# Half-height turns of k and q, q loaded eight tokens per row, and loads that wait for the fifth last

## The chip, the core and the metric

The kernel runs on one core of a Trainium2 chip. The core has a matrix engine (TensorE, PE in the profile; its weight loads are shown apart as PEld), a vector engine (VectorE, DVE), a scalar engine (ScalarE, ACT), a general engine (GpSimd, POOL) and a queue engine (SyncE, SP), which issues nearly all DMA transfers here. TensorE reads SBUF and writes PSUM, eight banks of 2 KB in each of 128 partitions; VectorE and ScalarE copy from PSUM to SBUF.

The metric is the device time of one execution, in microseconds (us), as the median of several runs. A profile is taken from one execution of its own.

## What is computed

A decayed linear attention in blocks of 64 tokens (4 batches, 8 heads, 768 tokens, 64 channels), and a highway layer on its output with the heads side by side (3072 tokens, 512 features):

```python
intra = np.einsum('bhic,bhjc->bhij', qb, kb) * Dmask[None]
intra = np.einsum('bhij,bhjd->bhid', intra, vb)
inter = np.einsum('bhid,bhde->bhie', qb * lam_pow[None], kv_state)
out[:, :, sl] = intra + inter
kv_state = lam_block[None, :, None, None] * kv_state + np.einsum('bhsd,bhse->bhde', kb_dec, vb)
...
H = np.maximum(x @ w_h, 0.0)
T = 1.0 / (1.0 + np.exp(-(x @ w_t + b_t)))
return (T * H + (1.0 - T) * x).astype(np.float32)
```

## The kernel before

The kernel works with chunks of 128 tokens in place of the 64 of the reference. The decay is split: q is multiplied by lam to the power of the token's position, v by its inverse, and a 0/1 mask (tri) is left between them. Two chunks are one superblock, n = 0 to 11, three to a batch.

The order of all work is written out by hand in PLAN (lines 17 to 60), a list of tokens. A loop at lines 384 to 388 reads each token and issues its instructions, so each engine gets its instructions in the order of the list. A token is name.arguments, with "=" before the PSUM banks and "@" before the engine. In the list:

- Lk, Lq, Lv (load, line 170): 256 KB of k, q or v, four heads of a superblock, on SP's queue. A partition holds two neighbouring tokens of each head, so one piece of a transfer is 512 bytes. W (line 176) loads a half of a weight matrix, in rows of 2 KB. WC casts it.
- CK, CQ, CV (lines 183, 193, 196): the cast of k to bf16, and the scaling of q and v with their powers. A last argument of 2 means all eight heads, 0 or 1 four of them.
- TK, TQ (trans, line 199): for each pair of heads and each of the two token parities, one 128 x 128 transpose on TensorE into one PSUM bank. EK, EQ (lines 206, 210) copy the 1024 columns out to kT and qT.
- S, SS (lines 236, 224): the scores, in 64 x 64 tiles of TensorE. SS mixes them with U, the state matmuls (line 219). KE copies the state out of PSUM. M (line 254) masks the scores on VectorE.
- I and A (lines 265, 276): the two parts of the attention's output, o. D (take, line 285) copies o out to xT. Its columns are in the order of parity, and the copy puts them in token order with a permuted write.
- F (block, line 295): eight matmuls of the highway layer, 256 tokens wide. H, G, X (lines 303, 308, 316): relu, sigmoid, gate.
- R (turns, line 340): turns of the result to token rows, in tiles of 64 rows; E copies them out, ST stores them through SP's queue. The last superblock goes in two chunks, with turn (line 321).
- Z (spin, line 362): matmuls without use that keep TensorE busy. PT (line 381) loads the sigmoid's table. B and BC make a column of the bias.

Each load needs a free buffer; there are five each of kf, qf and vf (BUFS, line 62). SP works its transfers in order, so a store whose data is not there yet holds the loads behind it. There is no other limit on transfers in flight.

Of the kernel before, what the change touches and what calls it, by code (L numbers as in the profile page):

```python
# [29 lines left out]
R.1=40 H.2.1 SS.3.1=62 Lv.5.0 F.2.0.0=3 CK.4.2@POOL KE.3.0@ACT M.3.1.1 Lv.5.1 E.1.1@ACT M.3.1.0 SS.3.0=52 E.1.0@ACT  # L30
H.2.0 Lq.6.0 TQ.4.2=0 KE.3.1@ACT CV.4.2@POOL M.3.0.1 TK.4.2=6 G.2.1@ACT Lq.6.1 F.2.0.1=4 M.3.0.0 EQ.4.2@ACT EK.4.2@DVE
Lv.6.0 I.3=32 A.3.0 CK.5.2@POOL A.3.1 Lk.6.1 SS.4.1=56 D.3.0@ACT D.3.1@DVE TK.5.2=0 KE.4.0@ACT M.4.1.1 Lk.6.0
F.3.0.0=2 G.2.0@ACT CQ.5.2@POOL EK.5.2@DVE Lv.6.1 SS.4.0=36 H.3.0 F.3.0.1=0 Lq.8.0 M.4.0.0 CV.5.2@POOL M.4.0.1
TQ.5.2=2 Lk.9.0 G.3.0@ACT F.3.1.0=3 X.2.1@DVE Lq.7.0 EQ.5.2@ACT X.2.0@DVE F.3.1.1=6 CQ.6.2@POOL M.4.1.0 Lq.7.1
KE.4.1@ACT I.4=14 H.3.1 G.3.1@ACT R.2=25 Lk.8.1 X.3.0@DVE A.4.0 E.2.1@ACT X.3.1@DVE A.4.1 Lk.7.1 SS.5.0=30 E.2.0@ACT
D.4.0@DVE CK.6.2@POOL SS.5.1=56 D.4.1@ACT Lk.7.0 TQ.6.2=2 M.5.0.0 KE.5.0@ACT CV.6.2@POOL TK.6.2=1 M.5.1.1 Lv.7.0
EQ.6.2@ACT F.4.1.0=4 M.5.0.1 Lv.7.1 EK.6.2@ACT F.4.0.0=3 H.4.1 Lk.8.0 M.5.1.0 I.5=62 SS.6.1=01 H.4.0 Lq.8.1 A.5.0
KE.6.0@ACT M.6.1.0 CQ.7.2@POOL R.3=45 Lv.9.1 A.5.1 M.6.1.1 SS.6.0=30 D.5.0@ACT Lv.8.0 F.4.0.1=1 M.6.0.0 D.5.1@ACT
M.6.0.1 Lk.9.1 TQ.7.2=6 G.4.0@ACT CK.7.2@POOL F.5.0.0=3 Lq.10.1 EQ.7.2@ACT F.4.1.1=2 H.5.0 Lk.10.1 E.3.1@ACT X.4.0@DVE
TK.7.2=0 CV.7.2@POOL G.4.1@ACT I.6=63 ST.0 KE.6.1@DVE F.5.0.1=5 X.4.1@DVE Lv.8.1 F.5.1.0=1 G.5.0@ACT CK.8.2@POOL  # L40
EK.7.2@DVE Lq.9.0 A.6.0 E.3.0@ACT H.5.1 A.6.1 SS.7.1=20 Lq.9.1 D.6.0@ACT D.6.1@DVE TK.8.2=4 M.7.1.1 F.6.1.0=1 Lv.9.0
EK.8.2@ACT X.5.0@DVE CK.9.2@POOL F.6.1.1=6 KE.7.0@DVE Lk.10.0 CQ.8.2@POOL H.6.1 R.4=30 SS.7.0=54 Lk.11.1 E.4.0@ACT
F.5.1.1=1 E.4.1@ACT M.7.0.1 G.6.1@ACT ST.4 M.7.1.0 TK.9.2=3 Lq.10.0 M.7.0.0 TQ.8.2=0 G.5.1@ACT CV.8.2@POOL F.6.0.0=4
EQ.8.2@DVE Lk.11.0 KE.7.1@ACT X.5.1@DVE I.7=25 EK.9.2@ACT Lq.11.0 A.7.0 H.6.0 A.7.1 CQ.9.2@POOL SS.8.0=01 X.6.1@DVE
D.7.1@ACT Lv.10.1 SS.8.1=34 M.8.0.1 D.7.0@ACT F.6.0.1=6 KE.8.0@DVE Lq.11.1 CK.10.2@POOL F.7.0.0=5 M.8.1.0 G.6.0@ACT
M.8.1.1 ST.3 TQ.9.2=1 CV.9.2@POOL H.7.0 F.7.1.0=2 EQ.9.2@ACT Lv.10.0 X.6.0@DVE TK.10.2=3 M.8.0.0 ST.1 I.8=45
EK.10.2@ACT CQ.10.2@POOL H.7.1 SS.9.1=61 A.8.1 KE.9.0@ACT M.9.1.0 A.8.0 R.5=02 M.9.1.1 SS.9.0=36 CK.11.2@POOL
E.5.1@DVE F.7.0.1=1 KE.9.1@ACT M.9.0.1 E.5.0@ACT F.7.1.1=2 D.8.0@DVE D.8.1@ACT ST.5 CQ.11.2@POOL M.9.0.0 G.7.0@ACT
Lv.11.1 TK.11.2=6 Lv.11.0 I.9=04 F.8.1.0=5 EK.11.2@ACT ST.2 X.7.0@DVE TQ.10.2=3 G.7.1@ACT H.8.1 CV.10.2@POOL F.8.0.0=1
EQ.10.2@ACT R.6=65 H.8.0 A.9.1 X.7.1@DVE A.9.0 SS.10.1=31 D.9.0@ACT D.9.1@DVE F.8.1.1=2 E.6.1@ACT M.10.1.1 F.9.1.0=0  # L50
E.6.0@DVE G.8.1@ACT M.10.1.0 ST.6 TQ.11.2=4 CV.11.2@POOL KE.10.0@DVE F.9.1.1=5 EQ.11.2@ACT X.8.1@DVE SS.10.0=16
G.9.1@ACT H.9.1 R.7=32 M.10.0.1 KE.10.1@ACT F.8.0.1=4 X.9.1@DVE E.7.0@ACT M.10.0.0 E.7.1@ACT I.10=06 SS.11.0=53
G.8.0@ACT ST.7 A.10.0 M.11.0.0 A.10.1 SS.11.1=21 D.10.1@ACT X.8.0@DVE F.9.0.0=5 KE.11.0@ACT M.11.1.0 D.10.0@ACT
F.9.0.1=6 M.11.0.1 M.11.1.1 F.10.1.0=4 G.9.0@ACT H.9.0 I.11=20 X.9.0@DVE A.11.0 A.11.1 R.8=31 D.11.0@ACT R.9=56
E.8.0@ACT F.10.0.0=2 E.9.0@DVE E.9.1@ACT E.8.1@ACT D.11.1@DVE ST.9 F.10.1.1=3 H.10.0 ST.8 F.10.0.1=6 H.10.1 G.10.1@ACT
F.12.1.1=5 G.10.0@ACT X.10.1@DVE F.11.1.1=1 F.11.1.0=0 G.12.1@ACT X.10.0@DVE F.11.0.1=2 G.11.1@ACT H.11.1 F.12.1.0=4
R.10=36 G.11.0@ACT H.12.1 X.11.1@DVE F.11.0.0=0 E.10.0@ACT X.12.1@DVE F.12.0.1=4 E.10.1@ACT H.11.0 F.12.0.0=1
G.12.0@ACT X.11.0@DVE ST.10 R.11.1.1=5 H.12.0 R.11.0.2=3 E.11.1.1@DVE X.12.0@DVE E.11.0.2@ACT ST.11.1.1 R.11.1.0=0
ST.11.0.2 E.11.1.0@DVE ST.11.1.0
"""  # L60

BUFS = dict(kf=5, qf=5, vf=5, kb=3, qb=2, vs=3, kT=2, qT=2, m=8, xT4=2, th4=2, xT2=3, xT1=2, th2=2, th1=2, hm2=3, hm1=2, tb2=2, tb1=2, ss=4, o=5, oh=2, oq=1)
# [3 lines left out]
def kernel(  # L66
# [13 lines left out]
    C = 128  # L80
# [4 lines left out]
    J = 2  # L85
    N = B * NST
# [12 lines left out]
    def copy(eng, dst, src):  # L99
        if eng == "ACT":  # L100
            A.activation(dst, src, AF.Copy)  # L101
        else:
            ENG[eng].tensor_copy(dst, src)  # L103
# [62 lines left out]


    SRC = {"k": k, "q": q, "v": v}

    def load(x, n, p, eng):  # L170
        b, c = divmod(n, NST)
        hs = heads(p)
# [246 lines left out]
```

## Time and profile before

| | |
|---|---|
| median of 7 runs | 109.19 us (108.9 to 111.0) |
| the profiled execution | 109.75 us |
| its span, first to last instruction | 107.7 us |
| TensorE busy, granted clock | 99.3 us, 0.998 |
| VectorE, ScalarE, GpSimd busy | 82.4, 71.8, 55.6 us |
| moved by DMA | 27.59 MB in 42701 packets, 256 GB/s mean |
| loads of k, q, v | 24 each, 5.3, 5.6, 5.4 us to landing (median) |

Busy times overlap between engines, and a busy engine is not always at its peak. The span is the profiled execution's own; what lies around it is not in the trace. In a list of groups, a row gives line, engine, operation, output and inputs with their shapes, the count, then the busy time in us and the mean of one in ns, then the idle time of the engine ahead of them and what ended it. In the chain by time, a row gives start, duration, and what ran.

### The profile page before, as it was taken

How to read it: one execution, taken by the hardware profiler on the slowest of the kernel's cores; microseconds unless marked ns; L12 is line 12 of the kernel's file. 1: busy time of each engine (PE TensorE's matmuls, PEld its weight loads, DVE VectorE, ACT ScalarE, POOL GpSimd, SP SyncE). 2: the span in 40 equal slices, each digit the busy share in tenths (PEclk: the TensorE clock that was granted, in tenths of full speed). 3: DMA queues.
4: the chain of work that ended last, by engine and by line, in shares of the span. 5: the costliest groups of instructions: out<-in, count | busy, mean ns of one | idle time of the engine just before them, and what ended most of it. 6: DMA issues, size and time to landing. Idle time of an engine off the chain costs nothing.

```text
span 107.7 us, 4970 instructions
## 1 busy us (share of the span) xinstructions
PE 99.3 (92%) x2190; PEld 80.5 (75%) x2190; DVE 82.4 (77%) x140; ACT 71.8 (67%) x129; POOL 55.6 (52%) x46
## 2 busy tenths in 40 slices
PE   4986999999999999999999999998899999999950
PEld 1332665588987888889889889896698888899930
DVE  1233495879798797999995996999577998958860
ACT  3304254686875598499679758978197798687940
POOL 6028340427989877889548396998193060000000
PEclk9999999999999999999999999999999999999999
DMA  0899999999999999999999999999749454108264
GB/s 3 231 303 291 291 355 389 321 288 268 279 304 287 301 280 293 280 291 282 293 290 300 308 359 303 338 313 344 257 169 277 161 202 163 42 6 318 78 242 147
DMA packets 42701, 27.59 MB, mean 256 GB/s; under 512 B 1588, under 2 KB 38712, under 8 KB 42680
## 3 DMA queue, kind: packets, MB, share of 16 engines
q1 hardware_dynamic: 42528, 27.27, 86.6%
q8 instruction: 17, 0.28, 1.2%
q14 instruction: 4, 0.03, 0.1%
q10 hardware_dynamic: 152, 0.01, 0.1%
HBM read 20.98 MB, written 6.29 MB: 253 GB/s over the span
## 4 chain that ended last, share of the span: by engine, by line
PE 78%; DVE 6%; DMA 5%; issue 3%; POOL 1%; SPq 1%; ACT 1%; POOLq 0%; DVEq 0%
PE bt L300 19%; PE bh L300 18%; PE bs L216 8%; PE bo L281 6%; PE bx L347 6%; PE bqtr L204 6%; DMA qf<-in_q_dram 5%; PE bktr L204 5%; PE bspin L366 5%; PE bo L271 4%; DVE m L255 4%; PE kv L221 2%; POOL qb L190 1%; DVE hm L305 1%; SPq L173 1%
## 5 line engine op out<-in xcount | busy, mean ns | idle before, releaser
L300 PEld LDWEIGHTS <-w_b 128*128 128x128 bf16 x416 | 36.4, 98 | 4.5
L255 DVE TENSOR_TENSOR m<-bs,tri 128x512 bf16<-128x512 f32 x48 | 31.0, 679 | 2.2 <-PE bs L216 1.9
L190 POOL TENSOR_TENSOR qb<-qf,pow_q 128x1024 bf16<-128x1024 f32 (+1 forms) x13 | 23.5, 1809 | 11.1 <-DMA qf<-in_q_dram 11.1
L314 ACT ACTIVATE bt<-bt,bt_col 128x256 f32<-128x256 f32 (+1 forms) x52 | 22.0, 432 | 5.6 <-PE bt L300 2.9
L300 PE MATMUL bh<-xT,w_b 128*128 128x256 bf16 (+1 forms) x208 | 25.0, 265 | 0.0
L300 PE MATMUL bt<-xT,w_b 128*128 128x256 bf16 (+1 forms) x208 | 24.5, 265 | 0.0
L190 POOL TENSOR_TENSOR vs<-vf,pow_v 128x1024 bf16<-128x1024 f32 x10 | 19.0, 1902 | 7.2 <-DMA vf<-in_v_dram 6.2
L305 DVE SCALAR_TENSOR_TENSOR hm<-bh,xT 128x512 bf16<-128x512 f32 (+1 forms) x26 | 16.5, 643 | 3.7 <-PE bh L300 2.2
L318 DVE TENSOR_TENSOR th<-bt,hm 128x512 bf16<-128x512 f32 (+1 forms) x26 | 16.4, 642 | 2.1 <-ACT bt L314 2.0
L101 ACT ACTIVATE xT<-bo 128x512 bf16<-128x512 f32 x16 | 11.6, 750 | 4.2 <-PE bo L281 4.2
L216 PE MATMUL bs<-qT,kT 64*64 64x128 bf16 x384 | 13.8, 218 | 0.3
L366 PE MATMUL bspin<-blank,id 128*128 128x512 bf16 x45 | 12.6, 424 | 1.4 <-POOL id masks.py:199 1.4
L101 ACT ACTIVATE ss<-kv 128x512 bf16<-128x512 f32 x15 | 8.9, 596 | 7.2 <-PE bs L216 6.0
L103 POOL CAST kb<-kf 128x1024 bf16<-128x1024 f32 (+1 forms) x10 | 9.9, 994 | 7.3 <-DMA kf<-in_k_dram 6.6
L216 PEld LDWEIGHTS <-kT 64*64 64x64 bf16 x384 | 10.9, 106 | 2.6 <-issue 1.1
L101 ACT ACTIVATE o<-bx 128x512 f32<-128x512 f32 x19 | 10.4, 596 | 1.4 <-PE bx L347 1.3
L101 ACT ACTIVATE qT<-bqtr 128x1024 bf16<-128x1024 bf16 (+1 forms) x10 | 9.8, 981 | 1.8 <-PE bqtr L204 1.8
L281 PE MATMUL bo<-m,vs 64*64 64x128 bf16 x384 | 9.3, 219 | 1.5 <-issue 1.1
L366 PEld LDWEIGHTS <-id 128*128 128x128 bf16 x45 | 4.4, 107 | 6.8 <-issue 2.2
L221 PE MATMUL kv<-vs,kb 64*64 64x64 bf16 x320 | 9.1, 196 | 0.0
L281 PEld LDWEIGHTS <-vs 64*64 64x64 bf16 x384 | 6.5, 106 | 3.3 <-issue 2.4
L204 PE MATMUL bqtr<-id,qb 128*128 128x128 bf16 x96 | 7.5, 220 | 0.9 <-POOL qb L190 0.9
(50 smaller groups left out, 109.0 us busy)
## 6 DMA issues: line engine op xcount, KB each, us to landing
kf<-in_k_dram SPq DMA_DIRECT2D x24, 256.0 KB, 5.3
vf<-in_v_dram SPq DMA_DIRECT2D x24, 256.0 KB, 5.4
qf<-in_q_dram SPq DMA_DIRECT2D x24, 256.0 KB, 5.6
out_dram<-o SPq DMA_DIRECT2D x11, 512.0 KB, 4.4
w_f<-in_moe_w_h_dram SPq DMA_DIRECT2D x2, 512.0 KB, 6.6
w_f<-in_moe_w_t_dram SPq DMA_DIRECT2D x2, 512.0 KB, 8.6
out_dram<-oh SPq DMA_DIRECT2D x2, 128.0 KB, 2.0
out_dram<-oq SPq DMA_DIRECT2D x1, 256.0 KB
```

Of the source, the lines that this page charges most:

```text
L101: A.activation(dst, src, AF.Copy)
L190: ENG[eng].tensor_tensor(dst, in0=get(src, n)[:, heads(p)].rearrange("p h (j d) -> p h j d", j=J), in1=pw[:, n % NST, heads(p), :, None].t ...
L204: T.transpose(t[:, i, j, :], get(x + "b", n)[:, j, h:h + 2, :], id128)
L216: T.matmul(get("s", n, e, hp // 2)[half(b), hp % 2, j, :], lhsT=get("kT", n)[half(e), hp, j, half(b)], rhs=get("qT", n)[half(e), hp, :, ha ...
L221: T.matmul(kv[half(e), hp, half(e)], lhsT=get("kb", n)[half(b), j, 2 * hp + e, :], rhs=get("vs", n)[half(b), 2 * hp + e, j, :], start=firs ...
L255: V.tensor_tensor(new(("m", n, e, u), [128, 2, J, C]), in0=get("s", n, e, u), in1=tri[:, None].to_broadcast([128, 2, J, C]), op=ALU.mult)
L281: T.matmul(get("o", n, b)[half(e), hp, :], lhsT=get("vs", n)[half(b), 2 * hp + e, j, :], rhs=get("m", n, e, u)[half(b), hp % 2, j, :], sta ...
L300: T.matmul(t[:, r, :], lhsT=w_b[w][:, kc, (2 * u + r) * 128:(2 * u + r + 1) * 128], rhs=get("xT", *g)[:, kc, :], start=(kc == 0), stop=(kc ...
L305: V.scalar_tensor_tensor(new(("hm", g, u), [128, 2, z * C], tag=f"hm{z}"), in0=get("h", g, u), scalar=0.0, in1=get("xT", *g)[:, 2 * u:2 * ...
L314: A.activation(dst[:, r, :], src[:, r, :], AF.Sigmoid, bias=bt_col[:, 2 * u + r:2 * u + r + 1])
L318: ENG[eng].tensor_tensor(new(("th", g), [128, NP, z * C], tag=f"th{z}")[:, 2 * u:2 * u + 2, :], in0=get("tt", g, u), in1=get("hm", g, u), ...
L366: T.matmul(t, lhsT=id128, rhs=blank, start=True, stop=True)
```

## The change

- A turn's input is now 64 rows (one chunk, b) instead of 128, so that there are twice as many, of half the size, alternating between the upper and the lower half of TensorE's rows. k and q of a superblock are turned by one token T, into two banks, one for each chunk; each bank holds k and q. A bank is copied out by ET (evac_t) with one copy for k and one for q, 512 columns each. TK and TQ stay for the first superblock, which is done in halves.
- q is loaded in rows of eight tokens: partition (o, h) holds tokens 8o to 8o+7 of the heads 2h and 2h+1, and one piece of a transfer is 2 KB. A load is one head parity; both are needed ahead of CQ. The powers for q are made anew for that layout (two small DMA and arithmetic steps at the start).
- The copy of q out of PSUM reads in runs of four and puts the columns in token order, four head pairs side by side for each token. So the moving operand of the scores and of I steps by four elements. With q in token order, o is too: D is a plain copy, and the mask is made for that order.
- All transfers on SP go through dma, which from the 15th on makes each wait for the fifth last.
- PLAN is written anew: other places, engines and banks of the tokens throughout. The engine counts: KE 20 on ScalarE (15 and 5 on VectorE before), ET 15 on ScalarE and 11 on VectorE, D 13 and 11 (16 and 8), E of whole superblocks 15 and 7 (19 and 3). The spins are 47 instead of 45. PT comes ahead of the first turn.

```diff
+    lam_bc = singles.tile([128, H + 2], F32)
+    A.dma_start(out=lam_bc[:, 0:H], in_=lam.partition_broadcast(128))
+    A.dma_start(out=lam_bc[:, H:H + 2], in_=lam.rearrange("(h x) -> h x", x=2)[None].to_broadcast([32, NP, 2]))
...
+    issued = []
+
+    def dma(dst, src, eng=None):
+        i = (eng or nc.sync).dma_start(out=dst, in_=src)
+        if len(issued) >= 14:
+            tc.add_manual_dep(i.ins, issued[-5].ins.name,
+                              mybir.DependencyInfo(mybir.DependencyClass.Sync, mybir.DependencyReason.DATA), reason="few transfers at a time")
+        issued.append(i)
 
     def load(x, n, p, eng):
         b, c = divmod(n, NST)
+        ts = slice(c * 2 * C, (c + 1) * 2 * C)
+        if x == "q":
+            dst = new(("qf", n), [128, 2, Q * D], F32)
+            dma(dst[:, p], q[b, :, ts, :].rearrange("(h x) (o j) d -> x o h (j d)", x=2, j=Q)[p])
+            return
...
+    def cast_q(n, p, eng):
+        js = slice(0, Q) if p == 2 else slice(4 * p, 4 * p + 4)
+        z = js.stop - js.start
+        ENG[eng].tensor_tensor(new(("qb", n), [128, Q, 2, D])[:, js].rearrange("p j x d -> p x j d"),
+                               in0=get("qf", n).rearrange("p x (j d) -> p x j d", j=Q)[:, :, js],
+                               in1=pow_q[:, n % NST, :, js, None].to_broadcast([128, 2, z, D]), op=ALU.mult)
...
-    def trans(x, n, p, bk):
+    def trans(xs, n, p, bk):
         hs = heads(p)
-        t = bank((x + "tr", n, p), bk[0], [128, (hs.stop - hs.start) // 2, J, C], BF16)
-        for i, h in enumerate(range(hs.start, hs.stop, 2)):
-            for j in range(J):
-                T.transpose(t[:, i, j, :], get(x + "b", n)[:, j, h:h + 2, :], id128)
...
+        for b, i in enumerate(bk):
+            bank(("tr", n, p, b), i, [128, 2, (hs.stop - hs.start) // 2 * C // 2 * J], BF16)
+        if "k" in xs:
+            t = [get("tr", n, p, b)[:, 0].rearrange("p (h j i) -> p h j i", j=J, i=C // 2) for b in range(2)]
+            for i, h in enumerate(range(hs.start, hs.stop, 2)):
+                for j in range(J):
+                    for b in range(2):
+                        T.transpose(t[b][:, i, j, :], get("kb", n)[half(b), j, h:h + 2, :], id128[half(b), half(b)])
+        if "q" in xs:
+            t = [get("tr", n, p, b)[:, 1].rearrange("p (j i) -> p j i", i=C // 2) for b in range(2)]
+            for i in range(Q if p == 2 else Q // 2):
+                for b in range(2):
+                    T.transpose(t[b][:, i, :], get("qb", n)[half(b), i + (4 if p == 1 else 0)], id128[half(b), half(b)])
+
+    def evac_t(n, p, b, eng):
+        es = slice(0, 512) if p == 2 else slice(256 * p, 256 * p + 256)
+        js = slice(0, Q) if p == 2 else slice(4 * p, 4 * p + 4)
+        dst, src = new(("T", n), [128, 2, 2, 512], tag="kT")[:, b], get("tr", n, p, b)
+        copy(eng, dst[:, 0, es], src[:, 0])
+        copy(eng, dst[:, 1].rearrange("p (i j h) -> p i j h", j=Q, h=NP)[:, :, js],
+             src[:, 1].rearrange("p (j i h) -> p i j h", i=16, h=NP))
+
+    def kT(n, b, hp):
+        return get("T", n)[:, b, 0].rearrange("p (h j i) -> p h j i", h=NP, j=J)[:, hp]
+
+    def qT(n, b, hp):
+        return get("T", n)[:, b, 1].rearrange("p (i h) -> p i h", h=NP)[:, :, hp]
...
     def score(n, e, hp, j, b):
-        T.matmul(get("s", n, e, hp // 2)[half(b), hp % 2, j, :], lhsT=get("kT", n)[half(e), hp, j, half(b)],
-                 rhs=get("qT", n)[half(e), hp, :, half(b)], start=True, stop=True)
+        T.matmul(get("s", n, e, hp // 2)[half(b), hp % 2, j, :], lhsT=kT(n, b, hp)[half(e), j, :],
+                 rhs=qT(n, b, hp)[half(e)], start=True, stop=True)
...
-        copy(eng, new(("xT", *g), [128, NP, z * C], tag=f"xT{z}")[:, :, r * C:(r + 1) * C].rearrange("p n (q j) -> p n j q", j=J),
-             get("o", n, b).rearrange("p n (j q) -> p n j q", j=J))
+        copy(eng, new(("xT", *g), [128, NP, z * C], tag=f"xT{z}")[:, :, r * C:(r + 1) * C], get("o", n, b))
```

The new PLAN's beginning, up to the first highway block:

```
Lk.0.1 Lq.0.0 Lq.2.1 Lq.1.1 Lq.1.0 Lq.0.1 Lk.0.0 Lk.1.1 Lk.1.0 Z.8=0 B=0 CK.0.1@ACT BC PT TK.0.1=12 Lv.0.0
Lv.0.1 CQ.1.2@POOL CQ.0.0@DVE Lv.1.0 CK.0.0@DVE Lv.1.1 Z.13=0 TQ.0.0=34 CQ.0.1@POOL TK.0.0 Lk.2.0 ET.0.0.1@DVE
Z.2=0 TQ.0.1 ET.0.1.1@ACT ET.0.1.0@DVE W.0.1 ET.0.0.0@ACT CK.1.2@ACT Z.6=0 S.0.1=56 W.0.0 S.0.0=04 M.0.0.1 CV.0.1@POOL
Lq.2.0 CV.0.0@DVE Lk.2.1 M.0.1.0 Z.7=1 U.0.0 T.1.2=12 CV.1.2@POOL M.0.0.0 Lv.2.1 KE.0.0@ACT M.0.1.1 ET.1.2.1@ACT Z.1=3
I.0=35 A.0.0 ET.1.2.0@DVE Lv.2.0 U.0.1 A.0.1 WC.0.1.1@ACT D.0.1@DVE KE.0.1@ACT W.1.1 D.0.0@ACT Z.6=0 SS.1.1=40
WC.0.0.1@POOL Lq.3.1 KE.1.0@ACT M.1.1.1 WC.0.1.0@POOL WC.0.0.0@DVE Z.4=1 SS.1.0=62 CQ.2.2@POOL Lq.3.0 I.1=15 M.1.0.0
F.0.0.0=3
```

In the dense part, from the first F to the last, the order on TensorE before changes the tile shape (128 x 128, 64 x 128, 64 x 64) 47 times, and the new one 59 times. There are ten sets of turns of a whole superblock in that part in both.

## The prediction

> **What bounds the kernel now.** I read the busy shares and the 40 slices first, then the chain of waits, then the groups of instructions, then busy time by stage.
>
> ```profile
> PE 99.3 (92%) x2190; PEld 80.5 (75%) x2190; DVE 82.4 (77%) x140; ACT 71.8 (67%) x129; POOL 55.6 (52%) x46
> PE   4986999999999999999999999998899999999950
> DMA  0899999999999999999999999999749454108264
> PE 78%; DVE 6%; DMA 5%; issue 3%; POOL 1%; SPq 1%; ACT 1%; POOLq 0%; DVEq 0%
> ```
>
> TensorE is nearly full from the fourth slice to the last but one, and it is 78% of the chain. The DMA row is as full until about 77 us, so two things are near their limits at once. Which one yields is seen in the chain by time:
>
> ```profile
> 45.58 0.45 PE bqtr L204 x8
> 46.03 0.87 PE bh L300 x8
> ...
> 74.87 1.05 issue
> ...
> 90.91 0.98 PE bh L300 x8
> 91.88 0.87 PE bt L300 x8
> ...
> 94.65 1.04 PE bx L347 x64
> ```
>
> From 22 us on the chain is TensorE's own stream; its longest plain gap is the 1.05. The pieces give a price list. Eight full turns (128 columns each) take 0.45. An FFN block takes 0.87, or 0.98 as the first after 64-row work: a change of tile shape costs 0.11. 64 half turns of the output, line 347, take 1.04 = 2 x 0.46 + 0.11, so 32 cost 0.46. By the same reading of other pieces, 32 score and state matmuls take 0.45, 16 intra matmuls 0.235, eight inter matmuls 0.45.
>
> Check: from the first FFN block (22.1 in the timeline) to the end of the last (102.06 + 0.61 = 102.7) the plan holds 41.8 of FFN, 8.6 of scores and states, 5.2 intra, 3.8 inter, 5.1 output turns, 20 x 0.45 = 9.0 of k and q turns, and 47 shape changes x 0.11 = 5.2: 78.7 of the 80.6 that passed. About 1.9 is idle. So this stretch is TensorE's.
>
> **Turns.** Per 256 tokens, two sets of eight 128-row turns become 32 turns of 64 rows and 64 columns. No row of before has a 64-row transpose; the nearest is line 347:
>
> ```profile
> L204 PE MATMUL bqtr<-id,qb 128*128 128x128 bf16 x96 | 7.5, 220 | 0.9 <-POOL qb L190 0.9
> L347 PE MATMUL bx<-id,xT 64*128 64x64 bf16 x176 | 6.6, 191 | 0.0
> ```
>
> It has the same 64*128 tile, 64 columns and alternation of halves. By it a set costs 0.46, not 0.90. Without overlap of the two halves each costs half of 0.45/8 = 0.056, so 32 cost 0.9 and nothing is saved. I take 0.46. In the dense stretch are ten sets: 9.0 becomes 4.6, -4.4. The new order changes shape 59 times, not 47: +1.3. Net -3.1, bounds +1.3 to -3.1.
>
> The busy table by stage shows a granted clock of 1.00 in every window from 10 to 101 us, turns included. [...]
>
> **Strided q.** q now lies interleaved by four heads in its turned tile, so the moving operand of every score and inter matmul steps by 8 bytes instead of 2. No matmul of before has a moving operand with such a step. At best it is free. [...] A score set already equals eight streams of 128 columns in one column half (8 x 0.056 = 0.45), so 24 score sets and ten inter sets gain 0.45 each: +15.3. Nothing in TensorE's full stream could hide that. I take the near end, 0, because every other moving operand here, whether in 64-element runs or 256 in a row, costs the same 0.42 to 0.44 ns a column, and keep +15.3.
>
> [...]
>
> **Copies out of PSUM.** Two copies of 1024 become four of 512. On ScalarE 1023 ns becomes 2 x 597, on VectorE 684 becomes 2 x 415:
>
> ```profile
> L101 ACT ACTIVATE qT<-bqtr 128x512 bf16<-128x512 bf16 x1 | 0.6, 597 | 0.6 <-PE bqtr L204 0.6
> L101 ACT ACTIVATE xT<-bo 128x512 bf16<-128x512 f32 x16 | 11.6, 750 | 4.2 <-PE bo L281 4.2
> L103 DVE CAST ss<-kv 128x512 bf16<-128x512 f32 x5 | 3.4, 680 | 0.2 <-PE kv L221 0.2
> ```
>
> The copies of o to xT lose their permuted write (750 against 596 for ss on ScalarE, 728 against 680 on VectorE). Counting the plan's tokens by engine with these rows, ScalarE ends at the same 72; VectorE gains 3.0 from turns, 2.8 from four output copies, 1.7 from three more xT copies, and loses 3.4 (ss, all to ScalarE now), 1.9 (vs), 1.4 (casts and the last half copies, net): +0.8. The q half reads PSUM in runs of four elements. Low bound 0; high bound VectorE at its fp32 rate, 680 for 415, over ten copies +2.6. I take 0. VectorE is busy 68.3 of the 79 us from 22 to 101 by stage, 86%; afterwards 68.7 of about 76, 91%; with the high bound 94%. TensorE hides it, but with less room: I raise the idle inside the dense stretch from 1.9 to 2.2, range 1 to 5.
>
> **Loads.** q arrives in rows of 2 KB, not 512 B. Stages with W (2 KB rows) against stages with q, k, v alone (last column GB/s):
>
> ```profile
> 17.00:18.00 1.00, 0.94 (x11) 0.53 (x9) 0.08 (x1) 0.33 (x1) 0.00 (x0) 1.00 0.98 371
> 18.00:19.00 1.00, 1.00 (x22) 0.47 (x19) 0.80 (x2) 0.00 (x0) 0.00 (x0) 1.00 1.06 382
> 40.00:50.00 10.00, 10.00 (x284) 8.86 (x281) 9.40 (x16) 8.08 (x17) 8.43 (x6) 1.00 1.05 287
> ```
>
> 6.29 MB at 287 is 21.9 us, at 376 16.7: 5.2 us of DMA time go, more than the 3.1 by which TensorE hurries. Without that cover the loads would hold TensorE at its old pace: up to +3.1.
>
> **The wait.** From the 15th transfer on, SP holds each until the fifth last has landed; behind it stand all later loads and stores, and for them wait POOL's casts. Before, a load landed in 5.3 to 5.6 us at one per 0.87 (the casts of the fourth to sixth load begin at 8.24, 9.01 and 9.97), so about six were in flight. With five, four still run (3.5 us of k and v, 2.7 of q) while the next is issued (0.5) and comes through (2.0, the store oh landing alone): no hole, price 0. Bounds: -0.9, one load's turn, if wanted loads share less; and if a lone load needed the 3.7 of lam, five would pass in 3.7 + 0.5, one per 0.84, which is the old pace: the 5.2 would be lost, and with it the cover, +3.1. The last stores find the fifth before them long landed.
>
> **Start and end.** By landings of 0.87 for k and v and 0.67 for q after the first at 5.5, q0 is whole at 8.9 and v0 at 13.2 (7.3 before). q0's second cast waits on POOL behind that of block 1 (8.2 to 10.1, then to 11.3), its turn and ScalarE's two copy pairs end at 13.5, scores follow, and masks start at 13.9 against 13.46. v0's scaling follows the first mask on VectorE, to 15.3; I count the state copy at 16.8, the first intra set at 17.3 (before 14.8, but its other half at 18.2), block 1's scores at 19.7 (19.3) and the first FFN block at 22.0 (22.1). W lands at 18.6, in time. The second load of lam (about 0.58 on ACT's queue) and the small setup steps (some 0.2 each) hide under the wait for q, and so does the sigmoid table (1.28 on ScalarE), which moves from 22.4 to about 6. Price 0, -1.5 to +1.5. At the end the last FFN block is followed by three VectorE steps of 0.42, a turn, a copy and the store, about 2.2 against 2.0: +0.2.
>
> **Sum.** 107.7 - 3.1 + 0.3 (idle) + 0.0 + 0.2 = 105.1. The profiled execution took 109.75 around its span of 107.7; the median is 109.19, so I add 1.5 to a span: 106.6.
>
> **Rivals.**
> 1. Strided reads slow TensorE (slower). It decides from 1.17 times on: 2.6 gained over 15.3. Doubled: 106.6 + 15.3 = 121.9; at half of that 114.2. Against it: all moving operands so far stream alike; for it: none of them steps. Chance 0.10.
> 2. The two halves of a turn do not overlap: 106.6 + 4.4 = 111.0. Against it, line 347's 0.46. Chance 0.07.
> 3. Loads or VectorE take over TensorE's bound and eat the gain: 106.6 + 3.1 = 109.7, less where they take part. For it: a full DMA row and VectorE at 91%; against it: 371 to 382 GB/s for 2 KB rows. Chance 0.15: 0.04 still faster, 0.07 no change, 0.04 slower.
> 4. The new order starts better than I count (-1.5) and idles less (-1.2): 103.9. Chance 0.14, part of faster.
>
> **Chances.** My forecast, 105 to 108.5, has 0.54. What can be told from no change is about 0.5%, 0.55 us. Faster: 0.54 + 0.14 + 0.04 = 0.72. Same: 0.07. Slower: 0.10 + 0.07 + 0.04 = 0.21. The range 103.4 to 111.0 leaves out rival 1 and a little at both ends; the forecast's own is 105 to 108.5.
>
> **What would show it.** Turn sets of 32 near 0.46; score sets still 0.45 and inter 0.45; about 59 shape steps of 0.11; W-like 370 GB/s when q passes; 512-element copies near 597 and 415; the first FFN block near 22.0; VectorE near 83 busy. Score sets above 0.55 would mean rival 1, turn sets near 0.9 rival 2, and TensorE idle before casts of q or k rival 3.

## The result and the profile after

| | before | after |
|---|---|---|
| median | 109.56 us (31 runs) | 122.36 us (121.75 to 123.24, 12 runs) |
| ratio, 95% interval | | 1.1204 [1.1171, 1.1236] |
| span of the profiled execution | 107.7 us | 120.6 us |
| first highway block starts (timeline) | 22.10 | 26.38 |
| last highway block ends | 102.7 | 114.9 |

The change costs 12% where 2.4% less was forecast. Ratios here leave disturbed executions out, so that a ratio can differ from the quotient of the two medians by about a per cent.

From the page of the changed kernel, the busy shares, two rows of the slices (tenths of 1/40 of the span) and the chain's shares:

```profile
PE 112.1 (93%) x2384; PEld 87.4 (72%) x2384; DVE 85.5 (71%) x156; ACT 70.2 (58%) x145; POOL 56.2 (47%) x47
PE   5649999999999999999999999999999999999950
DMA  2399999998999999999889000479996704004192
PE 89%; DMA 4%; ACT 2%; DVE 1%; issue 1%; ACTq 0%
```

TensorE is busy for 12.8 us more than before and has 89% of the chain instead of 78%. The other engines are busy within 3.1 us of what they were, and the row of DMA stands empty from about 66 us for the first time: the loads run ahead. Of the 12.9 us by which the span grew, 4.3 lie ahead of the first highway block, 8.0 between the first and the last (88.6 against 80.6), and 0.7 behind. TensorE's groups, one row for each shape, with the copies that feed it (busy us, mean ns of one, then idle ahead):

```profile
L261 PE MATMUL bs<-kT 64*64 64x128 bf16 x384 | 23.4, 289 | 0.0
L316 PE MATMUL bo<-kT,ss 128*128 128x128 bf16 x80 | 11.2, 292 | 0.0
L238 PE MATMUL btr<-id,kb 64*128 64x64 bf16 x192 | 5.1, 193 | 0.8 <-ACT kb L101 0.8
L243 PE MATMUL btr<-id,qb 64*128 64x64 bf16 x192 | 5.0, 190 | 0.0
L103 DVE COPY kT<-btr 128x512 bf16<-128x512 bf16 x18 | 6.6, 414 | 1.4 <-issue 1.1 <-PE btr L243 0.3
L101 ACT ACTIVATE kT<-btr 128x512 bf16<-128x512 bf16 x26 | 13.9, 600 | 5.1 <-PE btr L243 5.1
```

The first two rows are the score and inter matmuls, the only ones that read q in its turned form. Their tiles, shapes and counts are those of before:

```profile
L216 PE MATMUL bs<-qT,kT 64*64 64x128 bf16 x384 | 13.8, 218 | 0.3
L271 PE MATMUL bo<-qT,ss 128*128 128x128 bf16 x80 | 6.4, 219 | 0.0
```

They took 218 and 219 ns, busy 13.8 and 6.4 us; now it is 289 and 292, busy 23.4 and 11.2. The chain by time (start, duration, what) shows what that is for a set:

```profile
38.10 0.34 PE btr L238 x16
38.45 0.23 PE btr L243 x16
38.68 0.47 PE bx L391 x32
39.15 0.98 PE bh L344 x8
40.12 0.15 PE bs L261 x2
...
40.41 0.75 PE bs L261 x12
41.16 0.98 PE bh L344 x8
...
77.16 0.92 PE bo L316 x8
```

The turns are as cheap as predicted: 16 half turns of k in 0.34, of which 0.11 is the change of shape, and 16 of q in 0.23. The score set that starts at 40.12 takes 1.04 with its change of shape, 0.93 without, where it was 0.45. Eight inter matmuls take 0.92, where they took 0.45. Between the first and the last highway block the profile shows TensorE busy all the time, 88.6 us (26.38 to 114.95), so what is added there is TensorE's own.

### The profile page after: what moved, and what is told of

Its sections match the earlier page's. It is cut to its first block, busy times and chain, and to the rows that moved or that the text cites. A ratio compares the mean times of both kernels' runs of the same rounds, so it can differ in the third digit from the quotient of the medians.

```text
span 120.6 us, 5399 instructions
## 1 busy us (share of the span) xinstructions
PE 112.1 (93%) x2384; PEld 87.4 (72%) x2384; DVE 85.5 (71%) x156; ACT 70.2 (58%) x145; POOL 56.2 (47%) x47
## 3 DMA queue, kind: packets, MB, share of 16 engines
q1 hardware_dynamic: 33312, 27.27, 70.2%
## 4 chain that ended last, share of the span: by engine, by line
PE 89%; DMA 4%; ACT 2%; DVE 1%; issue 1%; ACTq 0%
PE bt L344 18%; PE bh L344 18%; PE bs L261 16%; PE bspin L410 9%; PE bo L316 8%; PE bo L326 6%; PE bx L391 5%; DMA lam_bc<-in_lam_dram 4%; PE btr L238 3%; PE btr L243 2%; PE kv L266 2%; ACT oh L101 1%; ACT kb L101 0%; ACTq L108 0%; DVE th L362 0%
## 5 line engine op out<-in xcount | busy, mean ns | idle before, releaser
L219 POOL TENSOR_TENSOR qb<-qf,pow_q 128x1024 bf16<-128x1024 f32 (+1 forms) x12 | 22.3, 1868 | 23.4 <-DMA qf<-in_q_dram 19.4
L225 POOL TENSOR_TENSOR vs<-vf,pow_v 128x1024 bf16<-128x1024 f32 (+1 forms) x12 | 22.0, 1830 | 8.6 <-issue 4.7
L261 PE MATMUL bs<-kT 64*64 64x128 bf16 x384 | 23.4, 289 | 0.0
L101 ACT ACTIVATE kT<-btr 128x512 bf16<-128x512 bf16 (+1 forms) x30 | 15.1, 572 | 10.6 <-PE btr L243 10.6
L101 ACT ACTIVATE ss<-kv 128x512 bf16<-128x512 f32 x20 | 11.9, 596 | 15.5 <-PE bs L261 12.6
L261 PEld LDWEIGHTS <-kT 64*64 64x64 bf16 x384 | 18.4, 119 | 3.4 <-issue 2.8
L362 DVE TENSOR_TENSOR th<-bt,hm 128x512 bf16<-128x512 f32 (+1 forms) x26 | 16.3, 641 | 1.6 <-ACT bt L358 1.6
L266 PE MATMUL kv<-vs,kb 64*64 64x64 bf16 x320 | 12.9, 201 | 0.0
L266 PEld LDWEIGHTS <-kb 64*64 64x64 bf16 x320 | 10.9, 107 | 0.4 <-issue 0.4
L316 PE MATMUL bo<-kT,ss 128*128 128x128 bf16 x80 | 11.2, 292 | 0.0
L103 POOL CAST kb<-kf 128x1024 bf16<-128x1024 f32 x9 | 9.3, 1036 | 3.2 <-ACT kT L101 1.8
L103 DVE CAST xT<-bo 128x512 bf16<-128x512 f32 x11 | 7.6, 687 | 4.2 <-PE bo L326 4.2
L101 ACT ACTIVATE xT<-bo 128x512 bf16<-128x512 f32 x13 | 7.5, 597 | 3.4 <-PE bo L326 3.4
(55 smaller groups left out, 102.7 us busy)
```

The source lines that it names most:

```text
L219: ENG[eng].tensor_tensor(new(("qb", n), [128, Q, 2, D])[:, js].rearrange("p j x d -> p x j d"), in0=get("qf", n).rearrange("p x (j d) -> p ...
L225: ENG[eng].tensor_tensor(new(("vs", n), [128, H, J, D])[:, heads(p)], in0=get("vf", n)[:, heads(p)].rearrange("p h (j d) -> p h j d", j=J) ...
L261: T.matmul(get("s", n, e, hp // 2)[half(b), hp % 2, j, :], lhsT=kT(n, b, hp)[half(e), j, :], rhs=qT(n, b, hp)[half(e)], start=True, stop=True)
L266: T.matmul(kv[half(e), hp, half(e)], lhsT=get("kb", n)[half(b), j, 2 * hp + e, :], rhs=get("vs", n)[half(b), 2 * hp + e, j, :], start=firs ...
L316: T.matmul(get("o", n, b)[:, hp, :], lhsT=get("ss", n, b)[:, hp, :], rhs=qT(n, b, hp), start=hp == 0, stop=False, skip_group_check=True)
```

## The experiments

Two theories at first. A: q's interleaving makes TensorE read its moving operand in steps of 8 bytes, and that halves its rate (the first rival of the prediction). B: something else that came with the change holds TensorE, such as the wait, the copies or the order of the work. In the expectations A is called theory S, and V (the wait) and L (the late start) are cases of B.

### contig_a, contig_b: q contiguous again

Two versions of the changed kernel lay q in token order head pair by head pair, so that moving operands are contiguous. They differ in what the copy out of PSUM steps over. The two copies are shown under one another, with a comment for each.

```diff
-        copy(eng, dst[:, 1].rearrange("p (i j h) -> p i j h", j=Q, h=NP)[:, :, js],
-             src[:, 1].rearrange("p (j i h) -> p i j h", i=16, h=NP))
+        # contig_a: writes in order, reads 128 bytes apart
+        copy(eng, dst[:, 1].rearrange("p (h i j) -> p h i j", j=Q, h=NP)[:, :, :, js],
+             src[:, 1].rearrange("p (j i h) -> p h i j", i=16, h=NP))
+        # contig_b: reads in runs of four, writes 256 bytes apart
+        copy(eng, dst[:, 1].rearrange("p (h i j) -> p i j h", j=Q, h=NP)[:, :, js],
+             src[:, 1].rearrange("p (j i h) -> p i j h", i=16, h=NP))
...
-        return get("T", n)[:, b, 1].rearrange("p (i h) -> p i h", h=NP)[:, :, hp]
+        return get("T", n)[:, b, 1].rearrange("p (h i) -> p h i", h=NP)[:, hp]
```

> The changed kernel, but q lies head pair by head pair in the turned tile, so that the moving operands of the scores and of the inter matmuls are contiguous again; the copy of q out of PSUM then writes in order and reads with its innermost step at 128 bytes. Theory S (the 8-byte step of the moving operand): a set of 32 score and state matmuls falls from 0.93 to 0.45 us, eight inter matmuls from 0.92 to 0.45, together about 13 to 15 us off the 122.4, so 107.5 to 110 if the dearer copies (up to 2.6 us more on VectorE) stay hidden. Rival V (loads held by the wait for the fifth last): no change, 122. Rival L (the late start, 4.5 us, has nothing to do with the step): at best 4.5 remain of the loss, 114.

Measured: 110.68 us (110.23 to 111.25), ratio 1.0155 [1.0106, 1.0203]. Groups of contig_a:

```profile
L261 PE MATMUL bs<-kT 64*64 64x128 bf16 x384 | 13.8, 218 | 0.3 <-issue 0.2
L316 PE MATMUL bo<-kT,ss 128*128 128x128 bf16 x80 | 6.5, 219 | 0.0
L103 DVE COPY kT<-btr 128x512 bf16<-128x512 bf16 x18 | 9.0, 546 | 0.3 <-PE btr L243 0.3
L101 ACT ACTIVATE kT<-btr 128x512 bf16<-128x512 bf16 x26 | 13.9, 605 | 3.9 <-DVE m L300 2.1 <-PE btr L243 1.8
```

The matmuls are back at 218 and 219 ns, and 11.7 of the 12.8 us are gone. The price moved, in part, to VectorE: its copies of k and q now take 546 ns in the mean, where they took 414, because q's half reads PSUM 128 bytes apart; on ScalarE that costs nothing (605 ns, where it was 600). The page's busy row and chain of contig_a:

```profile
PE 98.5 (91%) x2384; PEld 75.6 (70%) x2384; DVE 88.6 (82%) x156; ACT 69.7 (64%) x145; POOL 56.3 (52%) x47
PE 70%; DVE 15%; DMA 5%; issue 4%; ACT 2%; ACTq 0%; DVEq 0%
```

VectorE is on 15% of the chain now, so with the strided reads gone it is VectorE that ends some waits last.

> As the run before it, but the copy of q reads in runs of four as the changed kernel does, and writes with steps of 256 bytes. Theory S: the same matmul times, 0.45 a set; the total tells which order of the copy is cheaper, 107 to 111. Where a copy of 512 with such writes takes 0.75 us on ScalarE (the permuted write of the kernel before) instead of 0.60, 13 copies add 2 us to ScalarE, hidden. Rival V: 122.

Measured: 141.01 us, ratio 1.2813 [1.2717, 1.2908], though the matmuls are nearly right (226 and 238 ns). Groups of contig_b:

```profile
L101 ACT ACTIVATE kT<-btr 128x512 bf16<-128x512 bf16 x26 | 38.1, 1565 | 5.6 <-PE btr L243 5.5
L103 DVE COPY kT<-btr 128x512 bf16<-128x512 bf16 x18 | 24.9, 1442 | 0.7 <-issue 0.4 <-PE btr L243 0.3
```

A copy whose writes step by 256 bytes pulls the mean of the k and q copies to 1.4 and 1.6 us, and the score matmuls wait 16.3 us for them. The same bytes and the same engines, but steps on the writing side instead of the reading side. The widths differ as well (256 bytes against 128), so the side alone is not isolated.

### before_step: the step alone, in the old kernel

The kernel of before with nothing but q interleaved by its four head pairs.

```diff
-        copy(eng, new(("qT", n), [128, NP, J, C])[:, hs.start // 2:hs.stop // 2], get("qtr", n, p))
+        copy(eng, new(("qT", n), [128, J, C, NP])[:, :, :, hs.start // 2:hs.stop // 2].rearrange("p j c h -> p h j c"), get("qtr", n, p))
...
-                 rhs=get("qT", n)[half(e), hp, :, half(b)], start=True, stop=True)
+                 rhs=get("qT", n)[half(e), :, half(b), hp], start=True, stop=True)
```

> The kernel before, with one part of the change alone: q lies interleaved by four head pairs in its turned tile, so that the moving operands of the scores and inter matmuls step by 8 bytes. Turns, loads and order are those of before. Theory S: 24 sets of scores go from 0.45 to 0.93 and about ten of inter from 0.45 to 0.92: 109.5 + 14 to 16 = 123 to 126. Rivals V and L: 109.5, or up to 112 for copies whose writes step.

Measured: 130.01 us, ratio 1.1962 [1.1888, 1.2035], groups:

```profile
L216 PE MATMUL bs<-qT,kT 64*64 64x128 bf16 x384 | 24.1, 289 | 4.2 <-ACT qT L101 3.3 <-DVE qT L103 0.5 <-ACT kT L101 0.2
L101 ACT ACTIVATE qT<-bqtr 128x1024 bf16<-128x1024 bf16 x9 | 22.2, 2471 | 1.3 <-PE bqtr L204 1.2
```

The score matmuls take 289 ns as in the changed kernel, without its wait, loads or half turns: theory A. The time overshoots what I expected, and the second row says why. Here the copy has to write in steps of 8 bytes, and 1024 elements take ScalarE 2471 ns where they took 1023; the copies then hold TensorE as well (3.3 us of its wait for qT). The expectation had left that out.

### steps: what a step costs

Seven groups of 32 matmuls at the end of the old kernel, each with 128 moving columns that lie 1, 2, 3, 4, 6, 8 and 16 bf16 elements apart; the time of that run as a whole means nothing. The cut shows the loop of one group, with s for its step.

```diff
+        for _ in range(32):
+            T.matmul(t[:, 0:128], lhsT=id128, rhs=wide[:, 0:128 * s:s], start=True, stop=True)
```

> The kernel before, and behind its work seven groups of 32 matmuls of 128 columns each, one line of code to a group, whose moving operand steps by 1, 2, 3, 4, 6, 8 and 16 elements of two bytes. Its time says nothing. Theory S, by the changed kernel's eight inter matmuls in 0.92 us: 56 ns a matmul at step 1, 115 at step 4. [...]

TensorE's timeline of that kernel (start, duration), one row for each step in that order:

```profile
103.63 1.95 PE L366 MATMUL by<-wide,id 128*128 128x128 bf16 x32 [0.52 <-DVE oh L103]
105.41 2.01 PE L369 MATMUL by<-wide,id 128*128 128x128 bf16 x32
107.27 2.98 PE L372 MATMUL by<-wide,id 128*128 128x128 bf16 x32
110.08 3.88 PE L375 MATMUL by<-wide,id 128*128 128x128 bf16 x32
113.78 5.67 PE L378 MATMUL by<-wide,id 128*128 128x128 bf16 x32
119.28 7.43 PE L381 MATMUL by<-wide,id 128*128 128x128 bf16 x32
126.53 7.60 PE L384 MATMUL by<-wide,id 128*128 128x128 bf16 x32
```

From start to start, divided by 32, one matmul costs 56, 58, 88, 116, 172 and 227 ns for steps of 2, 4, 6, 8, 12 and 16 bytes; the last group, 32 bytes, about 230 (its 7.60 us less the 0.2 that the last matmul lasts beyond one such spacing: in the group before, 405 ns long and 227 apart). So a step of 4 bytes is free, 8 bytes cost twice as much, 16 bytes four times, and 32 bytes no more. The numbers from 6 to 16 bytes follow one rule: 128 columns at a step of s bytes pass over 8 x s pieces of 16 bytes (48, 64, 96, 128), and each such piece costs 1.8 ns. That 32 bytes cost no more than 16 is what makes the piece 16 bytes wide: from there on each column has a piece of its own.

One thing changes within the experiment, the clock that TensorE was granted. From the page, in 40 slices of 3.4 us:

```profile
PEclk9999999999999999999999999999999999955555
```

The run's mean clock of 0.939 over its span of 135.0 us, with 1.00 before the fall and 0.50 after it, puts the fall at about 118.5 us. So the groups up to 8 bytes ran at 1.00, and those of 16 and 32 bytes at 0.50. The last four matmuls of the 12-byte group (113.78 to 119.28, 172 ns apart in the mean) then ran at 0.50 too, and all 32 of it last 349 to 352 ns each: this price did not go with the granted clock. From that it is likely, but not shown, that 227 and 230 ns hold at 1.00 as well.

### pair2: a step of 4 bytes in the kernel itself

The changed kernel with heads interleaved by two pairs, the copy of q made in two parts.

```diff
+        for g in range(2):
+            copy(eng, dst[:, 1].rearrange("p (g i j e) -> p g i j e", j=Q, g=2, e=2)[:, g, :, js],
+                 src[:, 1].rearrange("p (j i g e) -> p g i j e", i=16, g=2, e=2)[:, g])
...
+        return get("T", n)[:, b, 1].rearrange("p (g i e) -> p g i e", g=2, e=2)[:, hp // 2, :, hp % 2]
```

> The changed kernel with q interleaved by two head pairs instead of four, so that the moving operand of score and inter matmuls steps by 4 bytes; each q copy becomes two of 256 elements. Theory (the step's bytes set the price, and 4 bytes are free): score and inter matmuls are back at about 220 ns, busy near 13.8 and 6.5, a score set takes 0.45; VectorE's pair of q copies costs about 2 x 0.28 where one cost 0.41, ScalarE's 2 x 0.38 where one cost 0.60; time 110 to 112, as with contiguous q. Rival (any step that is not 2 bytes, or the interleaving of different heads' rows as such, is slow): score matmuls near 250 to 290 ns, busy 18 to 23, time 116 to 122.

Measured: 112.13 us, ratio 1.027 [1.0199, 1.0341]; score matmuls 218 ns, busy 13.6, inter 219 ns, 6.6. The theory held for the matmuls and the rival fell: it is the width of the step and not the interleaving. The two short copies cost 2 x 282 ns on VectorE and 2 x 397 on ScalarE, so nothing is won over contig_a.

### no_wait: the wait alone

```diff
-        if len(issued) >= 14:
-            tc.add_manual_dep(i.ins, issued[-5].ins.name, ...)
```

> The changed kernel without the wait for the fifth last transfer. Theory S: 122.4, within 1 us, since TensorE has no gap while SP waits; loads land later each. Rival V: the loads were held, 4 us or more faster.

Measured: 122.31 us, ratio 1.1232 [1.1168, 1.1297], as with the wait. Yet the loads do run differently. Windows of the changed kernel (start:end, length, busy of PE, PEld, DVE, ACT and POOL with counts, granted clock, DMA share, GB/s), and below those of no_wait:

```profile
26.00:40.00 14.00, 14.00 (x293) 11.80 (x291) 10.90 (x20) 8.14 (x17) 9.79 (x7) 1.00 0.98 299
40.00:60.00 20.00, 20.00 (x491) 16.39 (x490) 16.99 (x30) 13.02 (x28) 14.09 (x10) 1.00 0.96 285
```

```profile
26.00:40.00 14.00, 14.00 (x309) 11.74 (x308) 10.73 (x21) 7.92 (x16) 10.25 (x7) 1.00 1.08 338
40.00:60.00 20.00, 20.00 (x488) 16.42 (x477) 17.15 (x31) 13.34 (x28) 13.74 (x10) 1.00 1.07 348
```

Five transfers in flight hold the loads at 285 to 299 GB/s; without the limit they run at 338 to 348. TensorE is full in both, so it costs nothing here.

### lam_one, best1: the late start

The first highway block comes at 26.38 in the changed kernel, 24.56 with contiguous q, 22.10 before. Windows of the changed kernel from 3 to 6 us:

```profile
3.00:4.00 1.00, 1.00 (x4) 0.33 (x3) 0.00 (x0) 1.00 (x1) 0.00 (x0) 1.00 0.38 93
4.00:5.00 1.00, 1.00 (x3) 0.11 (x1) 0.00 (x0) 0.03 (x1) 0.00 (x0) 1.00 0.10 25
5.00:6.00 1.00, 0.02 (x1) 0.00 (x0) 0.00 (x0) 0.00 (x0) 0.00 (x0) 1.00 0.51 151
```

Between 3 and 6 us the DMA engines move 93, 25 and 151 GB/s (82, 61 and 217 in contig_a); before, they moved 166, 282 and 336 there. The suspect is the second load of lam, which brings each of 128 partitions one piece of 8 bytes and is issued on ScalarE's queue at 1.28, among the first transfers. lam_one is contig_a without it; all of q gets the powers of heads 0 and 1.

```diff
-    A.dma_start(out=lam_bc[:, H:H + 2], in_=lam.rearrange("(h x) -> h x", x=2)[None].to_broadcast([32, NP, 2]))
+    V.tensor_copy(lam_bc[:, H:H + 2], lam_bc[:, 0:2])
```

> The changed kernel with contiguous q (as contig_a), but without the second load of lam; the powers of q are then those of heads 0 and 1 for all heads. Theory L1 (the 128 pieces of 8 bytes hold the transfers behind them): the hole of DMA from 3 to 6 us, where contig_a moved 61 to 217 GB/s, closes to 166 to 336 as in the kernel before, q is whole by about 7.5 instead of 9.3, and 0.5 to 2 us go, about 109. Rival L2 (five loads of q first is what is slow): the hole stays, 110.7.

Windows of lam_one:

```profile
3.00:4.00 1.00, 0.00 (x0) 0.00 (x0) 0.04 (x1) 0.15 (x1) 0.00 (x0) 1.00 0.82 235
4.00:5.00 1.00, 0.55 (x2) 0.25 (x2) 0.92 (x8) 0.21 (x1) 0.00 (x0) 1.00 1.08 374
5.00:6.00 1.00, 1.00 (x4) 0.29 (x2) 0.83 (x4) 0.74 (x3) 0.00 (x0) 1.00 1.02 346
```

The hole closes, and the first scaling of q starts at 7.73 where it started at 9.25 in contig_a. But the first highway block starts at 24.13, only 0.4 earlier, and the profiled execution takes 110.19. The gain shrank on VectorE: the first mask starts 1.2 earlier than in contig_a, the scaling of v behind it ends 0.7 earlier, and a cast of W 0.4 earlier. That cast takes 2.15 us here and 1.82 in contig_a, and 0.42 to 0.46 in the kernel before and in the changed one; what slowed it is not shown. VectorE's scalings take longer where GpSimd works beside them; from the timeline of the changed kernel (start, duration):

```profile
9.27 3.35 POOL L219 TENSOR_TENSOR qb<-qf,pow_q 128x1024 bf16<-128x1024 f32 x2 [6.42 <-DMA qf<-in_q_dram]
9.89 1.83 DVE L219 TENSOR_TENSOR qb<-qf,pow_q 128x512 bf16<-128x512 f32 x1 [2.28 <-issue]
...
17.19 0.68 DVE L225 TENSOR_TENSOR vs<-vf,pow_v 128x512 bf16<-128x512 f32 x1
```

The same operation and shape takes 1.83 us while GpSimd scales q, and 0.68 at 17.19, when GpSimd has nothing. These two products differ in the layout of their operands. The product at line 225 alone is the fairer pair: 0.68 us here, 1.17 in contig_a and 1.65 in lam_one, where GpSimd is still at work for the first 0.62 and 1.09 us of it. In both it ends about 0.55 us after GpSimd does, as if it had waited. My reckoning of the start had both engines at their undisturbed pace.

There is a third suspect, the spins. From the chain of the changed kernel:

```profile
8.22 5.19 PE bspin L410 x13
```

The run of 13 stands ahead of the first turn of q, which starts at 13.34, though VectorE had scaled its q at 11.72 (the k that is turned behind it was ready at 12.90). In lam_one the same run takes 3.06 us, and the turn starts 1.4 us after that scaling.

best1 is contig_a with those early pieces moved off VectorE, five spins fewer ahead of the first turn of q, and the copies E of the output turns all on ScalarE; the second load of lam stays.

```diff
-... CQ.1.2@POOL CQ.0.0@DVE Lv.1.0 CK.0.0@DVE Lv.1.1 Z.13=0 TQ.0.0=34 CQ.0.1@POOL TK.0.0
+... CQ.0.0@POOL CQ.0.1@POOL CQ.1.2@POOL Lv.1.0 CK.0.0@ACT Lv.1.1 Z.8=0 TQ.0.0=34 TK.0.0
-WC.0.0.1@POOL Lq.3.1 KE.1.0@ACT M.1.1.1 WC.0.1.0@POOL WC.0.0.0@DVE
+WC.0.0.1@POOL WC.0.0.0@ACT Lq.3.1 KE.1.0@ACT M.1.1.1 WC.0.1.0@POOL
```

> contig_a with its first scalings and casts moved: q of the first superblock on POOL ahead of the second's, the first k on ScalarE, one cast of W from VectorE to ScalarE, five spins fewer ahead of the first turn, and all seven output copies of VectorE on ScalarE. Theory: VectorE at 88.6 of 108.7 and its slow start are what is left over the kernel before; with about 7 us less of it and the first scores 1.5 to 2 us earlier the time is 106 to 108. Rival: the start hangs on the landings and the rest on TensorE alone: 110, no change.

Measured: ratio 1.0116 [1.0046, 1.0187], VectorE 79.8 us busy: no gain over contig_a that can be told. The first highway block starts at 24.09 in the profiled execution, which took 112.54 us.

### best2c, best3, best4, early_no_wait: all three suspects of the late start changed

best2c is contig_a with the early moves of best1, E as it was, spins cut (the runs of 13, 6, 7 and 6 ahead of the first highway block become 8, 4, 4 and 4), and each row's lam picked out of the first load:

```diff
-    A.dma_start(out=lam_bc[:, H:H + 2], in_=lam.rearrange("(h x) -> h x", x=2)[None].to_broadcast([32, NP, 2]))
...
+    V.tensor_tensor(sel, in0=row4_f.to_broadcast([128, NP]), in1=hp_f, op=ALU.is_equal)
...
+    V.tensor_tensor(ln_x, in0=ln_bc.rearrange("p (h x) -> p x h", x=2), in1=sel[:, None, :].to_broadcast([128, 2, NP]), op=ALU.mult)
+    V.tensor_reduce(ln_q, ln_x, axis=mybir.AxisListType.X, op=ALU.add)
```

> The changed kernel with contiguous q, without the second load of lam (each row's value is picked out of the first load on VectorE), with both first scalings of q on GpSimd, the second k cast and one W cast on ScalarE, and shorter runs of idle matmuls. Theory (the late start is the second lam load and VectorE working beside GpSimd): first FFN block near 21 to 22 us instead of 24, span about 105 to 106, time 106.5 to 108, faster than before. Rival (the start hangs on the landings of q and W, or the stretch after it has less slack than the start gave): first FFN block at 23.5 or later, or time 109.5 to 111.

Measured: 111.14 us, ratio 1.0124 [1.0054, 1.0193]. The first half of the theory held and the second half fell. The first highway block starts at 22.40, 2.2 earlier than in contig_a, and the last ends at 102.5 instead of 103.1: three quarters of what the start gave are handed back. Its chain:

```profile
DMA 50%; PE 26%; POOL 7%; SPq 7%; issue 3%; ACT 2%; DVE 0%; POOLq 0%
```

DMA now has half of it, and TensorE a quarter.

best3 is the same start with pair2's copies:

> The last kernel but one of this call's start (no second lam load, first scalings on GpSimd) with q interleaved by two head pairs. Theory: as contiguous q with that start, 106.5 to 108.5; the four extra short copies per block cost ScalarE and VectorE a little. Rival: 110 or more, because the copies of 256 elements make VectorE or ScalarE the bound.

Measured: 110.98 us, ratio 1.0176 [1.0116, 1.0236], first highway block at 21.82, DMA 41% of the chain: the rival's number, though not by the rival's cause, as VectorE is at 82.9 us and ScalarE at 72.2.

best4 is best2c with all E on ScalarE:

> As the contiguous-q kernel with the earlier start of this call, and all copies of the output turns on ScalarE. Theory (VectorE's load of about 88 us still costs idle TensorE time): 0.5 to 1 us faster than with the copies on both engines. Rival (TensorE's own stream bounds): the same within 0.5 us.

Measured: 112.43 us, ratio 1.019 [1.0116, 1.0264]. VectorE falls to 81.0 us and nothing is won: VectorE's total is not what holds best2c.

If loads hold best2c, the wait for the fifth last has a price there that it has not in the changed kernel. early_no_wait is best2c without it.

> The kernel with contiguous q and the earlier start (first FFN block at 22.40, 110.1 us, its chain half on loads) without the wait for the fifth last transfer. Theory (five transfers in flight hold the loads at 271 to 300 GB/s; without the wait the changed kernel's loads ran at 338 to 348 GB/s between 26 and 60 us, and only a kernel whose TensorE is ahead of its loads can gain from it): loads near 340 GB/s, TensorE's idle between 26 and 60 us falls from 1.55 to under 0.8 us, the loads leave the chain, span 106 to 107.3, time 107.5 to 108.8. Rival (the missing time is VectorE's and ScalarE's, not the loads'; or without the wait early loads share their bandwidth and the wanted ones come later, so that the start is lost again): time 109.5 to 111, the first FFN block at 23.5 or later or the chain on VectorE.

Measured: 110.67 us (12 runs), ratio 1.0089 [1.0042, 1.0137]. Windows of best2c, and below those of early_no_wait:

```profile
26.00:40.00 14.00, 12.95 (x285) 10.55 (x276) 12.82 (x22) 8.57 (x19) 9.22 (x6) 1.00 0.98 293
40.00:60.00 20.00, 19.50 (x568) 15.88 (x567) 19.26 (x35) 15.15 (x32) 15.30 (x11) 1.00 0.95 271
```

```profile
26.00:40.00 14.00, 13.96 (x329) 11.45 (x319) 13.44 (x24) 9.37 (x20) 10.84 (x7) 1.00 1.11 313
40.00:60.00 20.00, 19.70 (x580) 15.90 (x574) 19.25 (x35) 14.09 (x30) 17.64 (x12) 1.00 1.07 321
```

The loads speed up from 293 and 271 to 313 and 321 GB/s, TensorE's idle time from 26 to 60 us falls from 1.55 to 0.34 us, and no load is on the chain as far as it can be followed back (to 41.73 us), as the theory has it. But the time stays, by the rival's number, though neither of its signs came (first highway block at 22.11, VectorE 7% of the chain): of the 40 us from 60 to 100, TensorE now idles 2.0 where it idled 1.1 in best2c, and the last highway block ends at 102.3. VectorE is busy 19.25 of 20 us from 40 to 60 in both. No version that I ran beats the kernel before.

## Why the prediction was wrong

**Strided q: the step that failed.** The price was taken as 0, and the doubling kept as rival 1 with +15.3 and 121.9 us. The doubling is what happened: score sets 0.93, inter sets 0.92, and 122.36 us. The argument for the near end was that every moving operand of before costs 0.42 to 0.44 ns a column, "whether in 64-element runs or 256 in a row". But those runs are all contiguous inside; none of them bears on a step within a run, as the same paragraph says at its start. The far bound that it set aside pointed the right way: its +15.3 takes each of the 34 sets at twice its 0.45. No run ahead of the prediction shows that factor; the runs after it show 0.93 and 0.92 us a set, and 116 ns for 56 in the experiment on steps. That it came to two was luck. By the 1.8 ns, eight contiguous elements lie in a 16-byte piece and two at this step, a factor of four; half of it vanishes because 128 contiguous columns take TensorE 56 ns, not the 29 of their 16 pieces. A step of 4 bytes would have cost nothing and one of 16 four times (58 and 227 ns).

**Turns: right.** 0.34 and 0.23 for 32 half turns, 0.46 without the change of shape. Rival 2 falls. The granted clock reads 1.00 in the changed kernel's windows from 26 to 60 us, and the turns there keep their pace. The net of -3.1 shows in part: in contig_a, which keeps the half turns, the stretch from the first to the last highway block takes 78.5 us (TensorE busy for 77.6), where it took 80.6 (79.4) and 77.8 were forecast. With each matmul of the traces counted from its start to the next one's, turns fall from 9.0 to 5.6 us and intra from 7.8 to 6.3, but highway blocks rise from 43.1 to 44.6, scores and states from 9.8 to 11.0, and inter from 4.6 to 5.0. The 12 further changes of shape are among these rises, and so are short waits; the two were not told apart.

**Copies out of PSUM: right for the kernel as it is.** 414 and 600 ns for 415 and 597 forecast; reading in runs of four costs nothing. VectorE ended at 85.5 (forecast near 83), ScalarE at 70.2 (72).

**Loads and the wait: right in the time, wrong in part of the argument.** The price of the wait is 0 in the changed kernel (no_wait). But it rested on five transfers keeping the old pace with no hole, and on 2 KB rows bringing 5.2 us of cover. With the wait, loads run at 285 to 299 GB/s, no better than the 290 of before; only without it do they reach 338 to 348. The slow TensorE of the changed kernel hid that. In best2c it came to the surface as loads on half of the chain.

**Start: mis-sized.** Forecast 22.0 with -1.5 to +1.5, measured 26.38. About 1.8 of it goes with contiguous q (24.56). Of the other 2.6, best2c takes back 2.2 (22.40), near the 22.0. It changes three things: the second load of lam, which the prediction counted as 0.58 on ScalarE's queue and hid "under the wait for q"; VectorE's pieces beside GpSimd, priced from undisturbed rows; and the length of the spins, which the prediction did not price. The load alone gave 0.4 (lam_one 24.13), the moves with five spins fewer about 0.5 (best1 24.09). Shorter spins alone were not run, so what each is worth in the sum of three stays open.

**The sum with the failed step put right.** Forecast span 105.1. contig_a has 108.7: start +2.6, the stretch of highway blocks 78.5 instead of 77.8, end 5.6 instead of 5.2. The strided reads add 11.9 to that (120.6): 1.8 ahead of the first highway block and 10.0 in the stretch. The 15.3 counted all 24 score sets and ten inter sets of the kernel, but the stretch holds 20 and 8.5 of them (320 and 68 matmuls), by the measured prices 13.6. That 10.0 of these show fits waits of contig_a that a slower TensorE hides, 1.0 us of plain idle time among them; the rest of the 3.6 was not located. Priced right, the step would still not have put the forecast right: contig_a, the nearest to free strides, takes 110.7 (ratio 1.0155), out of the forecast's own range of 105 to 108.5. Its late start is one part of that, and its dearer copies on VectorE (15% of the chain, as rival 3 has it) another, so what truly free strides would have given is not shown.

**Open.** What holds TensorE to 80 us between the first and the last highway block in best2c and in early_no_wait, with loads in one and without in the other, is not settled. PLAN's order, written for another start, may be at fault; no run tests it. Half turns alone in the kernel before were not tried, since they need two banks for each set and so another plan.

## What to carry to other kernels

A layout is priced at its readers, not only at its writer: before a matmul's moving operand is interleaved, multiply the step into the sets that read it, and price a step that no row shows by its own small experiment or by the far bound, not by rows that share only the shape. On an engine that is full, a doubled small piece comes through for the most part (10.0 of 13.6 us here), while a saved one can be caught by the next limit (2.1 us came of the 2.8 forecast, and the late start took them back). And a wait or a slow load that costs nothing beside a slow engine (no_wait, 122.31 against 122.36) can stand on the chain once that engine is fast (best2c, DMA 50% of it).

## What the hardware showed

- TensorE's moving operand: 56, 58, 88, 116, 172, 227 and about 230 ns for 128 columns at steps of 2, 4, 6, 8, 12, 16 and 32 bytes, which is 1.8 ns for each 16-byte piece once that exceeds the 56. The granted clock was 1.00 up to 8 bytes and 0.50 at 16 and 32; within the 12-byte group (172) it fell from 1.00 to 0.50, and its 32 matmuls last 349 to 352 ns alike.
- Copies from PSUM to bf16: reads in runs of four elements free (414, 600 ns for 512, where contiguous ones took 415, 597); reads 128 bytes apart free on ScalarE (605), dearer on VectorE (the mean of k and q 546); writes in steps of 8 bytes 2471 ns instead of 1023 for 1024 elements on ScalarE, 2462 on VectorE.
- A load of 1 KB in pieces of 8 bytes, among the first transfers, goes with 82, 61 and 217 GB/s from 3 to 6 us (contig_a), 235, 374 and 346 without it (lam_one).
- VectorE beside GpSimd: 1.17 and 1.65 us (contig_a, lam_one) for a product of 512 columns that takes 0.68 alone (changed kernel). A cast that takes 0.42 to 0.46 in the kernel before and in the changed one took 1.82 and 2.15 in contig_a and lam_one; what slowed it is not shown.
